# The weights' largest values by a matmul with ones, raw weights loaded a matrix ahead, hints for the tails' branches, and the last tail at the end

## The chip, the core and the metric

The kernel runs on one core of one Trainium2 chip. Its time is that of one execution on the device, in microseconds (us). The time before is the median of three runs, and a profile is taken of one further execution. The core's engines are called TensorE or PE (matmuls; PEld is its weight load), VectorE or DVE, ScalarE or ACT, GpSimd or POOL, and SyncE or SP, which here only issues DMAs.

## What is computed

Attention without softmax over 8 batches, 8 heads, 576 positions and 64 columns per head, a norm, and then a mixture of 8 experts over the 4608 rows of 512 columns that come out, of which each row goes to two:

```python
kv = np.einsum('bhsd,bhse->bhde', k, v)
out = np.einsum('bhsd,bhde->bhse', q, kv)
rms = np.sqrt(np.mean(out * out, axis=-1, keepdims=True) + 1e-06)
x = out / rms * g_norm             # then as rows of 512
...
logits = x @ w_gate
noise_scale = np.log1p(np.exp(x @ w_noise))
noisy_logits = logits + noise_scale * noise
top2 = np.argpartition(-noisy_logits, 2, axis=1)[:, :2]
...                                 # top2_w: softmax over the two
for e in range(E):
    for k in range(2):
        mask = top2[:, k] == e
        h = np.maximum(x[mask] @ w1[e], 0.0)          # w1[e]: 512 x 1024
        out[mask] += top2_w[mask, k, None] * (h @ w2[e])   # w2[e]: 1024 x 512
```

## The kernel before, in words

**Attention** (0 to 206 us of the span). For each batch PE makes kv (L536), transposes it (L548), multiplies it with the gate's weights (L555) and then q with both (L565). A tile of 128 rows goes through six stages: s0 and s1 on ACT, s2 and s3 on ACT, DVE and POOL (L592 makes x on POOL), s5 stores x to xs in memory by a DMA that ACT issues (L601). So a late x on POOL holds ACT's queue, and what stands behind it there, kvT (L551) among others. The gate's steps run in chunks beside it (L129 to L200); in L142 to L148 DVE, ACT and POOL take turns, and PE needs the outcome gt_sel (L169) for the running counts (L179). Beside all that, expert 0's weights are made ready, and the first two units of expert 0 are begun.

**Experts** (from 206 us). An expert has 10 tiles of 128 slots. They are worked on in units: expert 0 has four full units of two tiles, the others two full units of four tiles; each expert then has a tail of the tiles 8 and 9, which are filled only in part. In the last expert the tail stands between the two full units. PE's order is written out by the loop at the end: l1 of unit u (x times w1), then l2 of unit u - 1 (h times w2). A full l1 of four tiles is 96 matmuls of 128 x 512 in f16 in eight steps of twelve, and so is its l2. A tail's l1 stands in a Switch of nine arms (called the up Switch here; L431, with the zero matmul L435 as first in each arm), one arm for each 32 columns that the expert needs; its l2 stands in a Switch of three (the down Switch). The numbers that choose the arm are loaded into PE's registers a unit ahead (RV). L893 is the Switch's own branching. At the head of an arm before already stands a hint for the arm's exit.

A unit's rows come by a gather (L344, POOL), are parted into two f16 halves, xh (L351 on ACT, L352 on POOL), and are transposed by DMAs that SP issues (xT, L364). After l1, ACT (L412) and DVE (L413) make hT of it. After l2, ACT makes y (L474) and POOL adds it to the output with an indirect DMA (L385), with a small memset, tick (L384), ahead of it.

**Weights.** While expert e is worked on, expert e + 1 is made ready in the background: fill() takes one step of locate(e + 1) and then of prepare(e + 1) at each yield of l1 and l2. locate makes the lists of rows: one-hots on DVE (L288 to L293), matmuls on PE (L301), and finish on DVE (L310 to L319). prepare makes the weights: for w1 and then for w2, SP loads 2 MB in four DMAs into the raw buffer rw (L251, L264), DVE takes the largest absolute value of each partition (mx, four reduces, L213), makes one number of each partition (sc, L215 and L217), and POOL takes the largest over the 128 partitions (al, L219). DVE makes a power of two of it (L221 to L227), and ACT and DVE (L241 to L246) part the scaled weights into two f16 halves, w1h and w1l. There is one raw buffer, so w2's load waits for the split of w1. All queues run in order, POOL's too: what stands behind L219 on POOL waits for it.

Of the kernel before, what the change touches and what calls it, by code (L numbers as in the profile page):

```python
# [9 lines left out]
F32 = mybir.dt.float32  # L10
# [5 lines left out]
OP = mybir.AluOpType  # L16
# [32 lines left out]
FE = 2  # L49
GB, HB = 6, 4  # L50
GRAIN, TY = 32, 4
PZ = 4
# [3 lines left out]
def attention_moe(ctx: ExitStack, tc: tile.TileContext, kvm, kvr, qt, gn, wgn, noise, w1, w2, out):  # L56
# [19 lines left out]
    ones = const.tile([P, P], BF, name="ones")  # L76
    V.memset(ones, 1.0)
    zrow = const.tile([P, DM], F32, name="zrow")
    V.memset(zrow, 0.0)
# [123 lines left out]

    WT = {}

    def weights(e, pool, lo, slack=0):
# [3 lines left out]
        def scale(o, src, mul):  # L210
# [7 lines left out]
            al = lists.tile([P, 1], F32, name="al")  # L218
            G.partition_all_reduce(al, sc[:, o:o + 1], channels=P, reduce_op=RED.max)  # L219
            yield  # L220
            V.tensor_scalar(al, al, 1e-30, 1e30, op0=OP.max, op1=OP.min)  # L221
            bi = lists.tile([P, 2], I32, name="bi")
# [25 lines left out]

        r1 = raw.tile([P, 4, 1024], F32, name="rw")
        for c in range(4):  # L250
            SP.dma_start(r1[:, c], w1[e, c * P:(c + 1) * P, :])  # L251
        yield WY
        for _ in range(slack):
            yield
        yield from scale(0, r1, gabs)
# [3 lines left out]
        for _ in range(min(slack, 3)):  # L259
            yield  # L260
        r2 = raw.tile([P, 4, 1024], F32, name="rw")
        v = w2[e].rearrange("(c f p) d -> c p f d", f=2, p=P)
        for c in range(4):
            SP.dma_start(r2[:, c].rearrange("p (f d) -> p f d", f=2), v[c])  # L264
        yield WY
        for _ in range(slack):
            yield
        yield from scale(3, r2, None)
# [3 lines left out]
        w["w2l"] = pool.tile([P, 4, FF], F16, name="w2l")  # L272
        yield from split(r2, w["w2h"], w["w2l"], sc[:, 4:5])
        for k in ("w2h", "w2l"):
            w[k] = w[k].rearrange("p c (f d) -> p (c f) d", f=2)
# [48 lines left out]
    for e in range(E):  # L324
        full = [[0, 1, 2, 3], [4, 5, 6, 7]] if e else [[2 * k, 2 * k + 1] for k in range(4)]
        tail = [(e, [8, 9], True)]
        full = [(e, t, False) for t in full]
        units += full + tail if e + 1 < E else full[:1] + tail + full[1:]
    XG, XT, HT, RV = {}, {}, {}, {}
    late = {}  # L330
    rot = [0]
# [62 lines left out]
    def l1(u):  # L394
# [35 lines left out]
        pss = [ps_tile([P, 2, 256]) for _ in range(4)]  # L430
        for arm in tc.Switch({ET.PE: RV[e][0]}, 256 // GRAIN + 1):  # L431
            n = arm * GRAIN
# [12 lines left out]
    def l2(u):  # L445
# [10 lines left out]
        if tail:  # L456
            pss = [ps_tile([P, DM]) for _ in tiles]
            for arm in tc.Switch({ET.PE: RV[e][1]}, len(tiles) + 1):
                for i, ps in enumerate(pss):
                    if i < arm:  # L460
                        mms(ps, i, range(8))
                    else:
                        T.matmul(ps, zero[:, 0:P], zero, start=True, stop=True)  # L463
# [256 lines left out]
    late["moe"] = after.enter_context(tc.tile_pool(name="moe_b", bufs=1))  # L720
    wts_b = after.enter_context(tc.tile_pool(name="wts_b", bufs=1))
    late["ps"] = ctx.enter_context(tc.tile_pool(name="psb", bufs=4, space=PSUM))
    psl = ctx.enter_context(tc.tile_pool(name="psl", bufs=1, space=PSUM))
# [71 lines left out]
    for u in range(EARLY, len(units) + 1):  # L795
        if u < len(units):
# [19 lines left out]
            todo = deque([halves, xpose] if u + 1 < len(units) and u + 1 not in XT else ())  # L816
            for i, _ in enumerate(l1(u)):
                fill()
                if todo and i >= XH:
                    todo.popleft()(u + 1)  # L820
            while todo:
                todo.popleft()(u + 1)
        if u > EARLY:
            for _ in l2(u - 1):
                fill()
# [71 lines left out]
```

## Time and profile before

| | |
|---|---|
| three runs | 1015.4, 1013.5, 1014.5 us |
| their median | 1014.5 us |
| the profiled execution | 1018.11 us, span 1016.3 us |
| mean granted clock of PE | 0.962 |
| PE busy | 916.7 us, 90% of the span |
| DVE, POOL, ACT busy | 491.0, 393.7, 330.9 us |
| moved by DMA | 146.01 MB, 144 GB/s on the mean |

The profile is of one execution, which took 3.6 us longer than the median of the runs. Busy times are those of the instructions alone; the idle time in front of an instruction is put down to what released it. A line number is one of kernel.py as printed above; a line such as L407 covers many matmuls, which differ in shape.

### The profile page before, as it was taken

How to read it: one execution, taken by the hardware profiler on the slowest of the kernel's cores; microseconds unless marked ns; L12 is line 12 of the kernel's file. 1: busy time of each engine (PE TensorE's matmuls, PEld its weight loads, DVE VectorE, ACT ScalarE, POOL GpSimd, SP SyncE). 2: the span in 40 equal slices, each digit the busy share in tenths (PEclk: the TensorE clock that was granted, in tenths of full speed). 3: DMA queues.
4: the chain of work that ended last, by engine and by line, in shares of the span. 5: the costliest groups of instructions: out<-in, count | busy, mean ns of one | idle time of the engine just before them, and what ended most of it. 6: DMA issues, size and time to landing. Idle time of an engine off the chain costs nothing. (4 is left out here: it accounts for less than half of the span.)

```text
span 1016.3 us, 15038 instructions
## 1 busy us (share of the span) xinstructions
PE 916.7 (90%) x5930; PEld 515.9 (51%) x5930; DVE 491.0 (48%) x1013; ACT 330.9 (33%) x573; POOL 393.7 (39%) x414
## 2 busy tenths in 40 slices
PE   9785877897879899999999999999998889998996
PEld 8674865584334544445444544464443344644442
DVE  2667998752735345454535443544255355411010
ACT  1645654222422242224323322332234223422221
POOL 0214454534441454236422552247213732452412
PEclk9995899998999999999999999999999999999998
DMA  9893986785563654554545474537255755462504
GB/s 344 300 349 132 335 283 225 226 168 125 120 108 109 160 81 95 146 126 97 114 103 155 97 127 94 163 79 145 44 141 131 137 93 170 91 116 56 94 10 59
DMA packets 140835, 146.01 MB, mean 144 GB/s; under 512 B 90785, under 2 KB 99105, under 8 KB 140705
## 3 DMA queue, kind: packets, MB, share of 16 engines
q1 hardware_dynamic: 108192, 82.25, 29.0%
q0 software_dynamic: 17920, 41.95, 22.2%
q10 hardware_dynamic: 14592, 19.93, 5.9%
q8 instruction: 99, 1.62, 0.7%
q14 instruction: 32, 0.25, 0.1%
HBM read 83.02 MB, written 40.11 MB: 121 GB/s over the span
## 5 line engine op out<-in xcount | busy, mean ns | idle before, releaser
L407 PE MATMUL pp<-xT,w1h 128*128 128x512 f16 (+5 forms) x1600 | 368.5, 328 | 20.2 <-DMA xT<-xh 14.1
L453 PE MATMUL pp<-w2h,hT 128*128 128x512 f16 x1200 | 364.0, 381 | 12.1 <-issue 4.6
L453 PEld LDWEIGHTS <-hT 128*128 128x128 f16 x1800 | 175.2, 98 | 226.0 <-issue 14.1
L413 DVE SCALAR_TENSOR_TENSOR hT<-pp,hT 128x512 f16<-128x512 f32 x160 | 107.4, 687 | 334.7 <-ACT hT L412 334.1
L407 PE MATMUL pp<-xT,w1l 128*128 128x512 f16 (+5 forms) x800 | 257.6, 327 | 0.0
L385 POOL DMA_INDIRECT out_rows<-y,row x80 | 133.6, 1670 | 255.5 <-ACT y L474 234.9
L453 PE MATMUL pp<-w2l,hT 128*128 128x512 f16 x600 | 228.7, 381 | 0.0
L407 PEld LDWEIGHTS <-w1h 128*128 128x128 f16 x1600 | 152.1, 100 | 128.1 <-issue 26.4
L412 ACT ACTIVATE hT<-pp 128x512 f16<-128x512 f32 x160 | 92.4, 597 | 302.0 <-PE pp L407 292.5
L352 POOL TENSOR_TENSOR xh<-xg,xh 128x512 f16<-128x512 f32 x80 | 113.6, 1444 | 115.5 <-ACT xh L351 93.4
L474 ACT ACTIVATE y<-pp,gate 128x512 f32<-128x512 f32 x80 | 53.7, 683 | 213.4 <-PE pp L453 198.1
L407 PEld LDWEIGHTS <-w1l 128*128 128x128 f16 x800 | 80.0, 100 | 56.0 <-issue 2.5
L213 DVE TENSOR_REDUCE mx<-rw 128x1 f32<-128x1024 f32 x64 | 76.8, 1215 | 63.3 <-DMA rw<-w 63.1
L344 POOL DMA_INDIRECT xg<-xs,idx x80 | 83.4, 1043 | 33.4 <-issue 21.7
L592 POOL TENSOR_TENSOR x<-o,ss 128x512 f32<-128x512 f32 x36 | 38.7, 1077 | 58.0 <-DVE ss L586 44.4
L565 PE MATMUL big<-kvbd,qt 128*128 128x160 f32 (+1 forms) x320 | 59.1, 335 | 1.9 <-ACT kvbd L557 1.9
L351 ACT ACTIVATE xh<-xg 128x512 f16<-128x512 f32 x80 | 46.7, 623 | 23.1 <-DMA xg<-xs,idx 16.0
L565 PEld LDWEIGHTS big<-kvbd,qt 128*128 128x128 f32 (+1 forms) x320 | 49.7, 200 | 4.6 <-ACT kvbd L557 3.0
L288 DVE TENSOR_TENSOR oa<-jb,lnb 128x1152 bf16<-128x1152 bf16 x32 | 50.9, 1591 | 0.6 <-PE M L301 0.6
L219 POOL PARTITION_ALL_REDUCE al<-sc x16 | 6.2, 390 | 115.4 <-DVE sc L217 73.9
L241 ACT ACTIVATE w1h<-rw,sc 128x1024 f16<-128x1024 f32 x32 | 34.9, 1139 | 30.1 <-DVE sc L227 30.0
L241 ACT ACTIVATE w2h<-rw,sc 128x1024 f16<-128x1024 f32 x32 | 35.0, 1137 | 24.5 <-DVE sc L224 24.5
(130 smaller groups left out, 594.0 us busy)
## 6 DMA issues: line engine op xcount, KB each, us to landing
rw<-w SPq DMA_DIRECT2D x64, 512.0 KB, 6.6
kvc<-kvm SPq DMA_DIRECT2D x32, 512.0 KB, 7.8
xs<-x ACTq DMA_DIRECT2D x36, 256.0 KB, 3.9
out_rows<-zrow ACTq DMA_DIRECT2D x36, 256.0 KB, 2.5
qt<-qt SPq DMA_DIRECT2D x8, 640.0 KB, 6.2
qt<-qt SPq DMA_DIRECT2D x8, 512.0 KB, 7.1
kvr<-kvr SPq DMA_DIRECT2D x4, 512.0 KB, 8.6
xg<-xs,idx POOLq DMA_INDIRECT x80, 4.1
```

The source lines that it names most:

```text
L213: V.tensor_reduce(mx[:, c:c + 1], src[:, c], axis=AX.X, op=OP.max, apply_absolute_value=True)
L241: A.activation(hi[:, c], src[:, c], AF.Copy, scale=s)
L288: V.tensor_tensor(oa, jb[:, None, :].to_broadcast([P, n, P]), lnb[:, s, e:e + 1].to_broadcast([P, n, P]), OP.is_equal)
L344: G.indirect_dma_start(out=x, out_offset=None, in_=src, in_offset=bass.IndirectOffsetOnAxis(ap=LI[e][:, t:t + 1], axis=0))
L352: G.tensor_tensor(x[:, 1], XG[u, t], x[:, 0], OP.subtract)
L385: d = G.indirect_dma_start(out=out, out_offset=bass.IndirectOffsetOnAxis(ap=LS[e][:, t:t + 1], axis=0), in_=y, in_offset=None, compute_op= ...
L407: T.matmul(ps[:, f % ps.shape[1], 0:n], w[wn][:, c, f * P:(f + 1) * P], x[:, xo + c, 0:n], start=(c == 0 and k == 0), stop=(c == HP - 1 an ...
L412: A.activation(h[:, 0, f:f + nf, 0:n], ps, AF.Relu)
L413: V.scalar_tensor_tensor(h[:, 1, f:f + nf, 0:n], ps, 0.0, h[:, 0, f:f + nf, 0:n], op0=OP.max, op1=OP.subtract)
L453: T.matmul(ps, h[:, hk, f, i * P:(i + 1) * P], w[wn][:, f], start=(f == 0 and k == 0), stop=(f == 7 and k == 2))
L474: A.activation(y, ps, AF.Copy, scale=LG[e][:, t:t + 1])
L565: T.matmul(TL[t, "ps"][r0:r0 + n, hp, 0:160], q[:, hp, s0 - o:s0 - o + n], kvbd[b % 2][:, hp, :], start=True, stop=True)
```

## The change

Five edits:

1. POOL's all-reduce over the partitions goes. DVE writes sc onto the diagonal of a 128 x 128 tile (dg = ident times sc), two background steps later PE multiplies a tile of ones (onef) with it, in f32, which gives each partition the whole row of 128 values, and a step later DVE takes the largest of these.
2. There are two raw buffers, one for w1 (pool raw) and one for w2 (raw_b). Both matrices of expert 1 are loaded right after attention. From then on w1 of expert e + 1 is loaded when w1 of expert e has been split, and w2 likewise, so each load goes out a matrix ahead of where it did.
3. The Switches carry labels, and switch_hint names them: at the sixth step of the l2 that stands before an up Switch, and at the sixth step of the l1 before a down Switch.
4. The last expert's tail stands behind both of its full units.
5. The buffers of xg are five instead of six. A dictionary moves up, and an import goes.

The diff, cut to its core:

```diff
@@ imports, constants
-from concourse.bass_isa import ReduceOp as RED
-GB, HB = 6, 4
-GRAIN, TY = 32, 4
+GB, HB = 5, 4
+GRAIN, TY, HINT = 32, 4, 5
+onef = const.tile([P, P], F32, name="onef")
+V.memset(onef, 1.0)
@@ before weights(), and in scale()
-    WT = {}
+    WT, RW, late = {}, {}, {}
+
+    def load_w1(e):
+        r = RW[e, 0] = raw.tile([P, 4, 1024], F32, name="rw")
+        for c in range(4):
+            SP.dma_start(r[:, c], w1[e, c * P:(c + 1) * P, :])
+
+    def load_w2(e):
+        r = RW[e, 1] = late.get("raw", raw).tile([P, 4, 1024], F32, name="rw")
+        v = w2[e].rearrange("(c f p) d -> c p f d", f=2, p=P)
+        for c in range(4):
+            SP.dma_start(r[:, c].rearrange("p (f d) -> p f d", f=2), v[c])
...
             al = lists.tile([P, 1], F32, name="al")
-            G.partition_all_reduce(al, sc[:, o:o + 1], channels=P, reduce_op=RED.max)
-            yield
+            dg = lists.tile([P, P], F32, name="dg", bufs=1)
+            V.tensor_scalar(dg, ident, sc[:, o:o + 1], None, op0=OP.mult)
+            yield
+            yield
+            ps = ps_tile([P, P])
+            T.matmul(ps, onef, dg, start=True, stop=True)
+            yield
+            V.tensor_reduce(al, ps, axis=AX.X, op=OP.max)
             V.tensor_scalar(al, al, 1e-30, 1e30, op0=OP.max, op1=OP.min)
@@ in weights(), behind split()
-        r1 = raw.tile([P, 4, 1024], F32, name="rw")
-        for c in range(4):
-            SP.dma_start(r1[:, c], w1[e, c * P:(c + 1) * P, :])
-        yield WY
-        for _ in range(slack):
-            yield
+        if (e, 0) not in RW:
+            load_w1(e)
+            yield WY
+            for _ in range(slack):
+                yield
+        r1 = RW.pop((e, 0))
         yield from scale(0, r1, gabs)
...
-        r2 = raw.tile([P, 4, 1024], F32, name="rw")
-        v = w2[e].rearrange("(c f p) d -> c p f d", f=2, p=P)
-        for c in range(4):
-            SP.dma_start(r2[:, c].rearrange("p (f d) -> p f d", f=2), v[c])
-        yield WY
-        for _ in range(slack):
-            yield
+        if (e, 1) not in RW:
+            load_w2(e)
+            yield WY
+            for _ in range(slack):
+                yield
+        elif e + 1 < E:
+            load_w1(e + 1)
+        r2 = RW.pop((e, 1))
         yield from scale(3, r2, None)
...
         yield from split(r2, w["w2h"], w["w2l"], sc[:, 4:5])
+        if "raw" in late and e + 1 < E:
+            load_w2(e + 1)
@@ units
-        units += full + tail if e + 1 < E else full[:1] + tail + full[1:]
+        units += full + tail
@@ l1(), l2()
-        for arm in tc.Switch({ET.PE: RV[e][0]}, 256 // GRAIN + 1):
+        for arm in tc.Switch({ET.PE: RV[e][0]}, 256 // GRAIN + 1, hint=f"up{e}"):
...
-            for arm in tc.Switch({ET.PE: RV[e][1]}, len(tiles) + 1):
+            for arm in tc.Switch({ET.PE: RV[e][1]}, len(tiles) + 1, hint=f"down{e}"):
@@ behind attention
+    late["raw"] = after.enter_context(tc.tile_pool(name="raw_b", bufs=1))
+    load_w1(1)
+    load_w2(1)
@@ the loop over the units
             for i, _ in enumerate(l1(u)):
+                if i == HINT and u and units[u - 1][2]:
+                    tc.switch_hint({ET.PE: RV[units[u - 1][0]][1]}, 3, label=f"down{units[u - 1][0]}")
                 fill()
...
-            for _ in l2(u - 1):
+            for i, _ in enumerate(l2(u - 1)):
+                if i == HINT and u + 1 < len(units) and units[u + 1][2]:
+                    en = units[u + 1][0]
+                    tc.switch_hint({ET.PE: RV[en][0]}, 256 // GRAIN + 1, label=f"up{en}")
+                if i == HINT and u + 1 == len(units):
+                    tc.switch_hint({ET.PE: RV[e][1]}, 3, label=f"down{e}")
                 fill()
```

On POOL, in attention, the rows of before from the first x on (L592 is x; L219 the all-reduce, whose ISA rows are its setup, as L147's is; L147 and L148 are the gate's):

```order
L592 TENSOR_TENSOR x<-o,ss 128x512
L219 ISA
L219 ISA al<-sc 128x1
L592 ISA
L592 TENSOR_TENSOR x<-o,ss 128x512 x8
L219 ISA
L219 ISA al<-sc 128x1
L147 ISA
L147 TENSOR_TENSOR gt_w<-gt_w,gt_nl 128x72
L148 TENSOR_TENSOR gt_w<-gt_w,nz 128x72
```

The same place on POOL in the changed kernel, where x is L612 and the gate's are L148 and L149:

```order
L528 MEMSET kvbd_162 128x640
L612 TENSOR_TENSOR x<-o,ss 128x512 x9
L148 TENSOR_TENSOR gt_w<-gt_w,gt_nl 128x72
L149 TENSOR_TENSOR gt_w<-gt_w,nz 128x72
L612 TENSOR_TENSOR x<-o,ss 128x512 x2
```

Both all-reduces and the setup rows around them are gone, and the x and the gate's instructions follow each other directly.

On SP, one expert's period among the experts, before (L364 is xT, two for a tail and eight for two full units; L251 and L264 are the loads of w1 and w2; L893 is a Switch):

```order
L364 DMA_TRANSPOSE xT<-xh 128x8x128 x2
L251 DMA rw<-w 128x1024 x4
L264 DMA rw<-w 128x2x512 x4
L893 UNCONDITIONAL_BRANCH
L364 DMA_TRANSPOSE xT<-xh 128x8x128 x8
L893 UNCONDITIONAL_BRANCH
```

and in the changed kernel (L384 is xT; L210 and L216 are the loads; L923 is a Switch):

```order
L384 DMA_TRANSPOSE xT<-xh 128x8x128 x2
L210 DMA rw<-w 128x1024 x4
L923 UNCONDITIONAL_BRANCH
L216 DMA rw<-w 128x2x512 x4
L384 DMA_TRANSPOSE xT<-xh 128x8x128 x8
L923 UNCONDITIONAL_BRANCH
```

The load of w2 has moved behind the up Switch, where it stands directly ahead of the eight transposes of the next full units; it is that of an expert later than before.

On PE, in the l1 of a second full unit of the changed kernel (L427 is the matmul of l1, L236 the one with ones):

```order
L427 LDWEIGHTS w1h
L427 MATMUL pp<-xT,w1h 128x512
L427 LDWEIGHTS w1l
L427 MATMUL pp<-xT,w1l 128x512
L236 MATMUL pp<-dg,onef 128x128
L427 LDWEIGHTS w1h
L427 MATMUL pp<-xT,w1h 128x512
```

Before, nothing of the weights' preparation stood on PE; now the matmul with ones stands between two of l1's steps.

On PE, in the l2 before an up Switch of the changed kernel (L473 is the matmul of l2, L852 the hint):

```order
L473 LDWEIGHTS hT
L473 MATMUL pp<-w2h,hT 128x512
L852 SWITCH_STRIDE
L852 ISA
L852 BRANCH_PREFETCH_HINT
L473 LDWEIGHTS hT
L473 MATMUL pp<-w2h,hT 128x512
```

The three rows of L852 are new. From them to the Switch itself there are 122 rows on PE, 61 matmuls with their weight loads.

More of the change, by code (lines that the diff above doesn't have):

```diff
@@ L327, in attention_moe @@
         full = [(e, t, False) for t in full]
-        units += full + tail if e + 1 < E else full[:1] + tail + full[1:]
+        units += full + tail
     XG, XT, HT, RV = {}, {}, {}, {}
-    late = {}
     rot = [0]
```

## The prediction

> **What bounds the kernel now.** I read the page's busy times, then the waits of PE in two stretches, then POOL's timeline at those waits, the records of the Switches' branches, and the granted clock in windows. On the page:
>
> ```profile
> span 1016.3 us, 15038 instructions
> PE 916.7 (90%) x5930; PEld 515.9 (51%) x5930; DVE 491.0 (48%) x1013; ACT 330.9 (33%) x573; POOL 393.7 (39%) x414
> ```
>
> PE is busy for 90%, so only its idle time and its slow time can be won. Waits of PE from 20 to 206 us (attention), in us, times, longest:
>
> ```profile
> PE RM L179 <- DVE gt_sel L169: 17.0, 2, 11.9
> PE kvt L555 <- ACT kvT L551: 11.8, 4, 6.9
> ```
>
> and from 206 to 1010 us (the experts):
>
> ```profile
> PE pp L407 <- DMA xT<-xh: 14.1, 3, 7.3
> PE pp L435 <- issue: 6.2, 3, 2.4
> PE pp L407 <- issue: 6.1, 4, 3.5
> PE pp L453 <- issue: 4.6, 2, 3.4
> PE pp L435 <- DVE mx L213: 4.5, 2, 2.4
> PE pp L453 <- ACT hT L412: 3.4, 2, 2.1
> PE M L301 <- DVE ob L293: 3.4, 1, 3.4
> PE pp L435 <- DVE sc L215: 2.7, 1, 2.7
> ```
>
> L435 is the first matmul in an arm of an up Switch. Its 13.4 us are three rows with three names; the names are chance, the place is one. Who is late in the other rows is seen on POOL (its timeline: start, duration, idle before):
>
> ```profile
> 34.72 0.38 POOL L219 PARTITION_ALL_REDUCE al<-sc  x1 [5.84 <-issue]
> 45.65 2.04 POOL L592 TENSOR_TENSOR x<-o,ss 128x512 f32<-128x512 f32 x2 [10.55 <-issue]
> 70.24 0.38 POOL L219 PARTITION_ALL_REDUCE al<-sc  x1 [9.10 <-issue]
> 79.64 0.33 POOL L147 TENSOR_TENSOR gt_w<-gt_w,gt_nl 128x72 f32<-128x72 f32 x1 [9.02 <-issue]
> 231.67 0.38 POOL L219 PARTITION_ALL_REDUCE al<-sc  x1 [7.02 <-issue]
> 239.12 2.98 POOL L352 TENSOR_TENSOR xh<-xg,xh 128x512 f16<-128x512 f32 x2 [7.07 <-ACT y L474]
> ```
>
> Each all-reduce itself takes 0.38 us, but POOL stands idle 6 to 9 us before it and 7 to 10.5 us behind it. The wait of 11.9 us follows the second, since L147, L148 and the chain to gt_sel come after it; the one of 6.9 us follows the first (x late, so ACT's store waits, and kvT stands behind it on ACT). The xT wait of 7.3 us follows the third: xh stands behind it on POOL, and SP's transpose behind xh.
>
> The Switches' branches (duration in ns, start):
>
> ```profile
> L893 PEldq COMPARE_BRANCH  x1: 6281/6281/6281, 342.6 to 342.6; - x1
> L893 PEldq COMPARE_BRANCH  x1: 3521/3521/3521, 395.9 to 395.9; - x1
> L893 PEldq COMPARE_BRANCH  x1: 301/301/301, 406.1 to 406.1; - x1
> ```
>
> The first is an up Switch, where PE then idles; the second a down Switch, whose 3.5 us lie under matmuls already queued (PE has no wait there); the third is an arm's exit, which already carries a hint at the arm's head, and takes 0.3 us. The two waits of L453 <- issue are the exits of expert 5's empty tail, too short for any hint: they stay.
>
> Waits cost twice: behind them PE runs at half clock (us, busy times of PE, PEld, DVE, ACT, POOL, granted clock, DMA share, GB/s):
>
> ```profile
> 49.40:54.40 5.00, 4.97 (x25) 4.86 (x26) 4.83 (x12) 3.17 (x9) 1.94 (x2) 0.50 0.28 97
> 85.00:88.50 3.50, 3.50 (x16) 2.95 (x16) 3.30 (x8) 3.47 (x7) 2.15 (x5) 0.50 0.40 150
> 242.20:249.00 6.80, 3.19 (x30) 3.12 (x30) 0.00 (x0) 0.00 (x0) 5.52 (x6) 0.50 1.18 204
> 300.20:307.00 6.80, 4.79 (x12) 1.75 (x13) 0.00 (x0) 0.00 (x0) 2.18 (x3) 0.50 0.71 143
> 559.60:563.00 3.40, 3.37 (x30) 3.26 (x31) 1.38 (x2) 0.00 (x0) 1.13 (x3) 0.50 0.63 84
> 798.50:801.90 3.40, 3.40 (x9) 1.18 (x8) 0.00 (x0) 0.55 (x1) 2.79 (x3) 0.50 1.09 149
> 100.00:125.00 25.00, 22.08 (x259) 20.01 (x259) 23.10 (x100) 15.27 (x41) 12.55 (x17) 0.82 0.91 323
> ```
>
> **Removing the all-reduce, attention.** The two waits, 11.9 + 6.9 = 18.8 us, end if POOL goes straight on. Half clock behind them: half of 5.0 and of 3.5, 4.3 us. Ceiling 23. What is late next are DVE and the DMA engines: in 100 to 125 us DVE is busy 23.1 of 25 us and the DMA share is 0.91, so work pulled forward meets full engines there. I take 18; the floor is 8, if that stretch takes back all but a third.
>
> **Removing it, experts.** Of the three xT waits (14.1) the smallest, 0.8, follows no all-reduce and stays, and of the 6.0 behind the second I leave 1.3 for branch and register loads that come with it: 12.0. The issue row's longest, 3.5, stands at 794 us behind another all-reduce, since its xh is late in the same way: together 15.5. The ob wait of 3.4 goes, since its chain on DVE stood behind the same result. Half clock: PE is busy 3.19 + 4.79 + 3.37 + 3.40 = 14.75 us in the four windows at 0.50, half of which is 7.4.
>
> The Trainium skill, "TensorE: Matmul & The Clock Gate", section "Part 1: The HAM clock gate", has the clock fall to half only after at least one idle window of about 3.4 us. The window at 559.6 follows a wait of 2.4 us alone, so the trace disagrees on that; by the page 1.7 us of the 7.4 would not be the wait's.
>
> **Hints.** The new hint stands at the sixth step of the l2 before an up Switch, some 60 matmuls ahead, where the branch took 6.3 us. If it is then like the hinted exit's 0.3 us, all 13.4 us of L435 go. The hint for the down Switch in the l1 wins nothing at its entry, which is hidden now; the two L453 waits at exits (3.4) I count as gone: they stand where an exit comes too soon after its hint, and with the tail's l2 now fetched ahead the sequencer is further in front. Experts' sum so far: 15.5 + 3.4 + 7.4 + 13.4 + 3.4 = 43.1 us.
>
> **What is added.** On PE, fourteen matmuls of 128 columns in f32 among the experts. The nearest row:
>
> ```profile
> 60.53 1.35 PE L565 MATMUL big<-kvbd,qt 128*128 128x160 f32 x8
> ```
>
> Each matmul is recorded twice there, so four in 1.35: 0.34 us for 160 columns, 0.27 for 128; 14 x 0.27 = 3.8. Below nothing it cannot be, since PE is the bound.
>
> PE is in order, so the matmul also waits for dg, and all of l1's steps are queued behind it. For w1 of each next expert this falls in the second full unit's l1, where locate's end stands ahead on DVE:
>
> ```profile
> 419.59 0.20 DVE L310 COPY m<-M 128x50 f32<-128x50 f32 x1
> 422.91 0.68 DVE L413 SCALAR_TENSOR_TENSOR hT<-pp,hT 128x512 f16<-128x512 f32 x1
> 424.16 0.69 DVE L413 SCALAR_TENSOR_TENSOR hT<-pp,hT 128x512 f16<-128x512 f32 x1 [0.56 <-ACT hT L412]
> 426.75 0.69 DVE L413 SCALAR_TENSOR_TENSOR hT<-pp,hT 128x512 f16<-128x512 f32 x1 [1.90 <-ACT hT L412]
> 430.40 0.68 DVE L413 SCALAR_TENSOR_TENSOR hT<-pp,hT 128x512 f16<-128x512 f32 x1
> 431.00 2.33 DVE L213 TENSOR_REDUCE mx<-rw 128x1 f32<-128x1024 f32 x2
> 433.25 0.68 DVE L413 SCALAR_TENSOR_TENSOR hT<-pp,hT 128x512 f16<-128x512 f32 x1
> 433.85 0.14 DVE L215 TENSOR_REDUCE sc<-mx 128x1 f32<-128x4 f32 x1
> ```
>
> A step of PE is 426.75 - 424.16 = 2.6 us. Raw weights are there early now, so DVE is the late one: locate's end 3.3 (419.59 to 422.91), hT 0.6, two reduces 2.3, hT 0.6, two reduces 2.3, hT 0.6, and about 0.6 for sc, gabs and dg (the first is 0.14): 10.3 us. It begins some 1.3 us (an ACT and a DVE hT, 0.6 + 0.7) behind its step on PE, and PE gets to the matmul four steps, 10.4, later. Wait 10.3 + 1.3 - 10.4 = 1.2 us, for six experts 7. It is nothing if locate's end is quicker than here, and up to 3 for each of all fourteen matmuls (a rival, below).
>
> **Raw weights ahead.** DVE's reduces no longer wait for loads; that is worth nothing on PE, where no wait of this kind stands outside the Switches. But SP's queue changes: the w2 load now goes out once the split of w2 is done, ahead of the eight transposes xT of the next expert's first full units. Its price as it stands:
>
> ```profile
> L264 SPq DMA_DIRECT2D rw<-w x4: 379/462/467, 441.9 to 443.3; - x4
> DMA to landing us min/median/max: 5.3/7.7/11.4
> 937.02 2.06 ACT L412 ACTIVATE hT<-pp 128x512 f16<-128x512 f32 x4 [6.16 <-PE pp L407]
> ```
>
> From 441.9 to the last landing 443.3 + 11.4 = 454.7 are 12.8 us. I estimate that it goes out some 5 us after a tail's arm ends (four hT, 2.1 us, then the rest of the split), so it is through at 18. The transposes land behind it, from about 21 to 23. PE needs them when the l2 that follows the arm is done: 96 matmuls, as in a full l1, so eight steps of 2.6, 20.8 us. So about 2 us a time for four experts: 8, from 0 (transposes pass the load) to 15.
>
> **Last tail at the end.** Its two y and scatters stand behind the last matmul instead of one. A scatter with its tick is about 2 us longer on POOL than the chain is now: 2, from 1 to 4. GB, late and the import cost nothing.
>
> **Sum.** Experts: 43.1 - 3.8 - 7 - 8 - 2 = 22.3. With attention's 18 it is 40 us. The profiled execution took 1018.1 us, so 978; the runs' median is 1014.5, 3.6 below it: 975 (974.5 rounded).
>
> **Rivals.**
> 1. The hints do nothing (the change doesn't do what it says). The sequencer runs through a hundred straight instructions between hint and branch and may lose the page fetched. Then 13.4 and 3.4 stay: 992. Against it: the hinted exit of 0.3 us lies 10 us behind its hint too. The Trainium skill, "Runtime: NRT & Kernel Launch", section "Instruction fetch mechanics", has the fetch purely sequential and each taken branch outside the window a forced fetch; by that rule this rival holds. The 0.3 us speaks against it. Chance 0.18.
> 2. Attention shortens by 8 only, since DVE and DMA are full at 100 to 125 us: 985. Chance 0.14.
> 3. Each of the fourteen scale matmuls waits 3 us for dg instead of the six with 1.2, because raw loads or hT hold DVE: 42 in place of 7, so 1010. For it: the same DVE queue takes hT for PE. Against: only w1's reduces stand behind locate. Chance 0.10.
> 4. Slower: the transposes stand behind the w2 load longer. The sum without (i.e. with the 8 given back) is 967; from 9.5 us a time for five experts it is 1014.5, and from there on the change loses. With 11 us a time, and 1.7 us of half clock behind each wait, it is 1030. Against it: the load would have to go out some 12.5 us behind the arm, or take 20 us where it took 12.8. Chance 0.03.
>
> **How the numbers follow.** The forecast, 975, has 0.55, and its own bounds are: below, no dg wait, no xT wait and attention's ceiling, 7 + 8 + 5 = 20, so 955, and 5 of scatter: 950; above, xT at 15 and dg doubled: 989. Rivals 1 and 2 lie within 998 with some 6 us of scatter; 3 and 4 are left out with 0.13. So 950 to 998. Two us, 0.2%, is about what a measurement of this kernel can tell from no change. All cases but the fourth are faster; from the third I give 0.02 to no change: faster 0.95, same 0.02, slower 0.03.
>
> **What would show it.** In the changed profile: no idle of 6 us on POOL in attention, and the gt_sel and kvT waits under 2 us; up Switches' branches at 0.3 us and no wait at the zero matmul; xT waits of about 2 us behind the up Switches; a wait of about 1 us at the scale matmul in the second full unit. Wrong it would be with branches of 6 us in the up Switches, with waits of over 2 us at scale matmuls, or with xT waits of 5 us and more.

## The result and the profile after

The changed kernel takes 1018.86 us, the median of 20 runs (1007.36 to 1026.38), and the kernel before, beside it on the same chips, 1010.31 us, the median of 20 as well (1004.85 to 1015.4). The ratio is 1.007, with a 95% interval of 1.0047 to 1.0093: the change makes the kernel slower, and the forecast was 975. The ratios here and below are estimates with their intervals, not quotients of the medians, and leave out slow executions, of which the changed kernel has three (the profiled one is among them). The profiled executions stand above these medians, before by 7.8 us (1018.11) and after by 4.6 (1023.48), so differences between the two traces are read by stage and not from the ends.

The page of the changed kernel, its span and busy times:

```profile
span 1021.6 us, 15198 instructions
PE 920.9 (90%) x5962; PEld 516.6 (51%) x5962; DVE 497.8 (49%) x1046; ACT 331.1 (32%) x573; POOL 379.6 (37%) x398
```

PE's share is the same 90%: what the edits took away in waits came back as other waits. Those of 20 to 206 us, in us, times, longest:

```profile
PE big L585 <- ACT kvbd L577: 12.5, 4, 9.9
PE kvt L575 <- ACT kvT L571: 6.4, 5, 2.0
PE RM L180 <- DVE gt_sel L170: 5.1, 1, 5.1
```

and those from 206 us on:

```profile
PE pp L427 <- DMA xT<-xh: 28.7, 5, 8.2
PE pp L236 <- DVE dg L232: 8.6, 6, 1.5
PE pp L427 <- issue: 5.1, 3, 2.5
PE pp L236 <- DVE hT L433: 3.6, 1, 3.6
PE pp L455 <- DVE dg L232: 1.5, 1, 1.5
```

The waits of 11.9 us (gt_sel) and 6.9 us (kvT) are gone, but a new one of 9.9 us stands in attention, and the first unit behind attention starts only 4.7 us earlier (at 201.5 us instead of 206.2). Among the experts the zero matmuls (L455) wait for 1.5 us in place of 13.4; the matmul with ones waits 8.6 us in six places; and the waits for xT have doubled, to 28.7 us. The branch of an up Switch where PE waited before, in ns:

```profile
L923 PEldq COMPARE_BRANCH  x1: 308/308/308, 440.6 to 440.6; - x1
```

So the hint does what it says there, and it does so at the other up Switches from 327 us on, which take 0.31 to 0.41 us (expert 5's, whose tail is empty, takes 0.3 us without a hint as well). It does not at the first, in expert 0, where it stands only 2.4 us ahead of the Switch:

```profile
L923 PEldq COMPARE_BRANCH  x1: 4994/4994/4994, 229.9 to 229.9; - x1
```

Four of the five xT waits, 6.8, 6.4, 8.2 and 5.3 us, stand behind the load of w2 (the fifth, 2.1 us at 259, does not). This is seen on SP's DMA issues at 570 us (issue, duration; then how long from issue to landing, min, median, max), first the load, then the transposes behind it, then four transposes that stand behind no load:

```profile
L216 SPq DMA_DIRECT2D rw<-w x4: 379/468/469, 569.8 to 571.2; - x4
DMA to landing us min/median/max: 3.7/5.1/6.5
...
L384 SPq DMA_TRANSPOSE xT<-xh x4: 1573/3242/5116, 571.8 to 580.1; - x4
PE pp L427: 8.2, 1
DMA to landing us min/median/max: 8.0/11.5/12.1
...
L384 SPq DMA_TRANSPOSE xT<-xh x4: 1232/1250/1287, 604.8 to 609.8; - x4
DMA to landing us min/median/max: 3.1/3.2/3.2
```

Behind the load a transpose takes 11.5 us to land instead of 3.2, and even its issue takes 3.2 us instead of 1.25. The fourth is issued at 580.1 and lands 12.1 us later, at 592.2; PE, at 584.2, waits for it for 8.2 us. The DMA queues (packets, MB, share of the 16 engines) show what runs meanwhile; q1 carries what SP issues, q0 the scatters and gathers that POOL issues. In the changed kernel, 569.7 to 578:

```profile
q1 hardware_dynamic: 1505, 2.20, 88.0%
```

and 578 to 592.3:

```profile
q1 hardware_dynamic: 3807, 0.94, 74.5%
q0 software_dynamic: 597, 1.17, 49.3%
```

In the kernel before, at the same place, 577 to 584.4:

```profile
q1 hardware_dynamic: 4083, 1.02, 71.7%
```

The load's 2 MB go first; about a tenth of the four transposes' 1 MB has moved by 578. The rest takes 14 us beside scatters and gathers, where before all of it took 7 us with no other queue at work, since the scatters came behind it. A packet of the transposes takes some 45 ns instead of 21 (an estimate: share times 16 engines times the stretch, by the packets). So the load has an effect that outlasts it: it moves the transposes to where they meet the scatters.

And PE pays again (us, busy times, granted clock), in the four windows behind the waits of 5 to 8 us; the fifth window follows a wait of 2.5 us (L427 <- issue), the last two follow waits of 1.5 and 1.4 us at the matmul with ones:

```profile
365.90:369.40 3.50, 3.50 (x9) 1.24 (x9) 0.00 (x0) 0.00 (x0) 0.88 (x1) 0.50 0.86 319
480.00:483.50 3.50, 3.50 (x9) 1.18 (x8) 0.00 (x0) 0.00 (x0) 0.95 (x1) 0.50 0.80 286
592.40:595.80 3.40, 3.40 (x9) 1.20 (x10) 0.00 (x0) 0.00 (x0) 0.00 (x0) 0.50 0.66 260
700.60:704.00 3.40, 3.40 (x9) 1.18 (x8) 0.00 (x0) 0.00 (x0) 1.90 (x2) 0.50 0.83 253
804.90:808.30 3.40, 3.40 (x10) 1.20 (x9) 0.00 (x0) 0.24 (x1) 2.48 (x4) 0.50 0.92 196
533.70:537.00 3.30, 3.30 (x16) 1.65 (x17) 1.39 (x7) 0.22 (x1) 0.00 (x0) 1.00 0.00 0
850.40:853.00 2.60, 2.60 (x13) 1.31 (x14) 1.34 (x7) 0.00 (x0) 0.00 (x0) 1.00 0.00 0
```

Half clock behind the four xT waits costs half of 13.8, 6.9 us. The new wait in attention begins on DVE (start, duration, idle before):

```profile
64.58 1.22 DVE L225 TENSOR_REDUCE mx<-rw 128x1 f32<-128x1024 f32 x1 [9.45 <-DMA rw<-w]
```

DVE comes to the reduce of expert 0's w2 at 55.1 us, before the load is issued, and stands there for 9.45 us, with ACT and PE behind it. In the trace of before the load went out at 51.4 and DVE came to it at 57.6, with no wait:

```profile
51.44 3.00 SPq L264 DMA_DIRECT2D rw<-w  x4
57.57 1.21 DVE L213 TENSOR_REDUCE mx<-rw 128x1 f32<-128x1024 f32 x1
```

In the changed kernel it goes out at 55.6:

```profile
55.59 3.86 SPq L216 DMA_DIRECT2D rw<-w  x4
```

It stands two steps later in the program, since scale has two more yields, and so behind the next batch's loads of k and v on SP, while POOL, no longer held, lets DVE arrive earlier. Two runs below bear out that the yields do this: in the kernel before with the first edit alone the loads of k and v go out at 46.1 us, w2's at 54.4, and DVE waits for it for 8.25 us; with the all-reduce and its single yield back, w2's load goes out at 50.5, ahead of those of k and v at 55.4.

### The profile page after: what moved, and what is told of

The parts are those of the page before. It is cut to its first block, busy times and chain, and to the rows that moved or that the text cites. A ratio compares the mean times of both kernels' runs of the same rounds, so it can differ in the third digit from the quotient of the medians.

```text
span 1021.6 us, 15198 instructions
## 1 busy us (share of the span) xinstructions
PE 920.9 (90%) x5962; PEld 516.6 (51%) x5962; DVE 497.8 (49%) x1046; ACT 331.1 (32%) x573; POOL 379.6 (37%) x398
## 5 line engine op out<-in xcount | busy, mean ns | idle before, releaser
L427 PE MATMUL pp<-xT,w1h 128*128 128x512 f16 (+5 forms) x1600 | 370.2, 329 | 36.1 <-DMA xT<-xh 28.7
L473 PE MATMUL pp<-w2h,hT 128*128 128x512 f16 x1200 | 364.8, 381 | 1.9 <-ACT hT L432 1.2
L473 PEld LDWEIGHTS <-hT 128*128 128x128 f16 x1800 | 176.0, 98 | 212.8 <-issue 5.4
L405 POOL DMA_INDIRECT out_rows<-y,row x80 | 130.1, 1626 | 371.5 <-ACT y L494 354.6
L427 PE MATMUL pp<-xT,w1l 128*128 128x512 f16 (+5 forms) x800 | 257.5, 328 | 0.0
L473 PE MATMUL pp<-w2l,hT 128*128 128x512 f16 x600 | 228.7, 381 | 0.0
L427 PEld LDWEIGHTS <-w1h 128*128 128x128 f16 x1600 | 150.6, 99 | 147.2 <-issue 49.4
L427 PEld LDWEIGHTS <-w1l 128*128 128x128 f16 x800 | 79.5, 99 | 58.0 <-issue 5.8
L364 POOL DMA_INDIRECT xg<-xs,idx x80 | 79.9, 998 | 35.1 <-issue 23.0
L225 DVE TENSOR_REDUCE mx<-rw 128x1 f32<-128x1024 f32 x64 | 74.4, 1208 | 11.3 <-DMA rw<-w 11.3
L612 POOL TENSOR_TENSOR x<-o,ss 128x512 f32<-128x512 f32 x36 | 38.6, 1073 | 64.6 <-DVE ss L606 57.4
L585 PEld LDWEIGHTS big<-kvbd,qt 128*128 128x128 f32 (+1 forms) x320 | 49.3, 201 | 17.3 <-ACT kvbd L577 13.4
L404 POOL MEMSET tick<- 1x1 f32 x80 | 37.2, 465 | 0.0
```

What stands on the lines that cost most here:

```text
L225: V.tensor_reduce(mx[:, c:c + 1], src[:, c], axis=AX.X, op=OP.max, apply_absolute_value=True)
L364: G.indirect_dma_start(out=x, out_offset=None, in_=src, in_offset=bass.IndirectOffsetOnAxis(ap=LI[e][:, t:t + 1], axis=0))
L405: d = G.indirect_dma_start(out=out, out_offset=bass.IndirectOffsetOnAxis(ap=LS[e][:, t:t + 1], axis=0), in_=y, in_offset=None, compute_op= ...
L427: T.matmul(ps[:, f % ps.shape[1], 0:n], w[wn][:, c, f * P:(f + 1) * P], x[:, xo + c, 0:n], start=(c == 0 and k == 0), stop=(c == HP - 1 an ...
L473: T.matmul(ps, h[:, hk, f, i * P:(i + 1) * P], w[wn][:, f], start=(f == 0 and k == 0), stop=(f == 7 and k == 2))
L585: T.matmul(TL[t, "ps"][r0:r0 + n, hp, 0:160], q[:, hp, s0 - o:s0 - o + n], kvbd[b % 2][:, hp, :], start=True, stop=True)
```

## The experiments

The kernel before was timed beside each; its median there was 1007.6 to 1012.4 us, so a difference of a few us between two experiments is uncertain unless the ratios show it too. The theory after the traces: the loss among the experts is the second edit's load of w2 ahead of the transposes; attention's lost gain is the load of expert 0's w2; the first, third and fourth edit are sound. The rivals are in the expectations. In each diff the changed kernel is the base, unless it says otherwise.

**w2's load put behind the transposes**, at the head of weights(e), ahead of w1's reduces:

```diff
         yield from split(r2, w["w2h"], w["w2l"], sc[:, 4:5])
-        if "raw" in late and e + 1 < E:
-            load_w2(e + 1)
...
+        if "raw" in late and (e, 1) not in RW:
+            load_w2(e)
         r1 = RW.pop((e, 0))
```

> The changed kernel, with the load of w2 of expert e+1 issued at the start of weights(e+1), behind the transposes, instead of ahead of them. Theory (the transposes queue behind that load on SP): PE's waits for xT fall from 28.7 us to under 4, the half clock behind them goes, and the time falls by about 33 us. Rival (the transposes are slow because scatters and gathers share the DMA engines then): xT waits stay over 15 us, and the time falls by less than 12 us.

982.16 us, ratio to before 0.9723 (0.9663 to 0.9784), 36.7 us under the changed kernel. Its waits for xT:

```profile
PE pp L236 <- DVE dg L232: 8.6, 6, 1.6
PE pp L427 <- DMA xT<-xh: 3.5, 1, 3.5
```

One issue moved by half an expert is worth 25.2 us of waits and the half clock behind them. The theory holds as to what has to move. It doesn't say by which way the load hinders the transposes, and it doesn't exclude the rival's scatters and gathers: with the load moved, the transposes run ahead of the scatters again, as in the kernel before.

**Six more steps in attention before the reduce of w2.**

```diff
             load_w2(e)
             yield WY
-            for _ in range(slack):
+            for _ in range(slack + 6):
                 yield
```

> The changed kernel, with six more steps between expert 0's load of w2 and its first reduce, in attention. Theory (DVE stands at the reduce for a load that is not there yet, 9.5 us, and PE behind it): that wait of DVE and PE's 9.9 us at 70 us go, and the time falls by about 10 us. Rival (attention is bound by its loads by then): the wait comes back elsewhere in attention, and the time falls by 3 us or less.

1035.89 us, ratio 1.024 (1.0176 to 1.0305): a miss, 17 us slower than the changed kernel. In its trace attention's wait of 9.9 us is gone, and the kernel is 7 us ahead at 228 us; then the xT waits are

```profile
PE pp L427 <- DMA xT<-xh: 47.8, 5, 20.8
```

instead of 28.7, with one of 20.8 us. How long the transposes take behind the load thus differs from kernel to kernel, and what makes it 20.8 us there isn't shown. The edit has to be judged where they don't, below.

**The same load from ACT's queue.**

```diff
-            SP.dma_start(r[:, c].rearrange("p (f d) -> p f d", f=2), v[c])
+            (A if "raw" in late and e > 1 else SP).dma_start(r[:, c].rearrange("p (f d) -> p f d", f=2), v[c])
```

> The changed kernel, with the load of w2 ahead issued by ACT instead of SP, at the same place of the program, so at about the same time. Theory A (the transposes only stand behind the load in SP's queue): xT waits fall under 6 us and the time falls by 25 us or more, as with the load put behind. Theory B (the load takes the DMA engines that the transposes need, whatever the queue): xT waits stay over 15 us, and the time falls by less than 12 us.

1006.83 us, ratio 0.9978 (0.9945 to 1.0012), 12 us under the changed kernel by the medians and 9 by the ratios, with xT waits of 19.0 us in its list. By these totals theory B holds; place by place it is between the two. Four transposes right behind the load, now on another queue, one expert ahead of the place shown above:

```profile
L384 SPq DMA_TRANSPOSE xT<-xh x4: 1263/1752/3267, 469.0 to 475.1; - x4
DMA to landing us min/median/max: 4.9/5.5/5.8
```

5.5 us to landing, against 3.2 alone and 11.5 behind the load on the same queue. The four waits that were 6.8, 6.4, 8.2 and 5.3 us are 2.5, 0.5, 2.5 and 0.9 us here, but a fifth, 2.1 before, is 15.2 us. There the last transpose was issued at 256.3, in the midst of the four loads (255.3 to 256.8), and landed at 272.0; from 262 us on scatters and gathers were under way as well. So both rivals have a part: the order in SP's queue has the larger one in four places, and sharing the DMA engines, without that order, can hold a transpose for 15.7 us. How much of this is the load and how much the scatters and gathers stays open; beside scatters alone, at 475 to 481 us, the transposes of the rows above kept landing in 5 to 6 us.

**Without hints, and the hints alone.** The changed kernel without the labels and the three switch_hint calls, of which the diff shows one:

```diff
-        for arm in tc.Switch({ET.PE: RV[e][0]}, 256 // GRAIN + 1, hint=f"up{e}"):
+        for arm in tc.Switch({ET.PE: RV[e][0]}, 256 // GRAIN + 1):
...
-                if i == HINT and u + 1 < len(units) and units[u + 1][2]:
-                    en = units[u + 1][0]
-                    tc.switch_hint({ET.PE: RV[en][0]}, 256 // GRAIN + 1, label=f"up{en}")
```

> The changed kernel without the three switch_hint calls and the labels. Theory (the hint makes the branch short): up Switches' branches take 4 to 6 us again, PE waits about 10 to 13 us at the zero matmuls, and the time rises by 10 to 17 us. Rival (the branches were long only because w2's load ran at the same time, and it doesn't now): branches under 3.6 us, hidden, and a time within 4 us of the changed kernel.

1032.3 us, ratio 1.0232 (1.0155 to 1.0309), 13 us slower, but not for the reason that was expected. An up Switch's branch there:

```profile
L916 PEldq COMPARE_BRANCH  x1: 3707/3707/3707, 561.7 to 561.7; - x1
```

3.7 us, hidden: PE waits 1.3 us at the zero matmuls. The xT waits are 32.4 us instead of 28.7, and the exits wait some 5 us; the rest of the 13 us stays open. By its time the rival fails too, which allowed 4 us. About the entry it fits: without w2's load beside them the up Switches' branches of the experts 1 to 4 and 6 take 3.3 to 3.7 us, and with it, in the kernel before, 5.7 to 6.3. The kernel before with the labels and the first two hint calls alone (base: the kernel before, with L435 and L453 as before and L898 as the Switch):

```diff
-            for _ in l2(u - 1):
+            for i, _ in enumerate(l2(u - 1)):
+                if i == HINT and u + 1 < len(units) and units[u + 1][2]:
+                    en = units[u + 1][0]
+                    tc.switch_hint({ET.PE: RV[en][0]}, 256 // GRAIN + 1, label=f"up{en}")
                 fill()
```

> The kernel before with the labels and the hints alone. If the hint makes the branch short also beside w2's load: no wait at the zero matmuls (L435, 13.4 us before) and a time 10 to 17 us below before. If it does not there: within 4 us of before.

986.26 us, ratio 0.9813 (0.9719 to 0.9906), 23 us faster by the medians, more than expected, but by the interval anything from 9 to 28 us. Its branch at an up Switch, beside w2's load:

```profile
L898 PEldq COMPARE_BRANCH  x1: 312/312/312, 437.8 to 437.8; - x1
```

Of the five up Switches that took 5.7 to 6.3 us, three are like this. At the other two the branch takes 3.1 and 3.8 us although its hint stands some 13 us ahead, one of them:

```profile
L898 PEldq COMPARE_BRANCH  x1: 3818/3818/3818, 637.0 to 637.0; - x1
```

PE has no wait there either. Its waits at the zero matmuls from 325 us on:

```profile
PE pp L435 <- issue: 1.2, 1, 1.2
PE pp L435 <- PE pp L453: 0.2, 1, 0.2
```

Of the 13.4 us 1.4 are left, and the half clock that followed is gone. The xT wait of 6.1 us at 302, behind a down Switch, is 2.3 here. Not all of the 23 us need be the hints': in the trace the first unit behind attention starts at 202.2 us instead of 206.2, and no hint stands ahead of it. The first edit alone loses, as shown below, and the fourth is worth little; the second was not run alone. So of the edits that were, the third is the only gain.

**No load ahead.** The changed kernel without its second edit: no raw_b, no load_w1 and load_w2 after attention, none ahead in weights().

```diff
-    late["raw"] = after.enter_context(tc.tile_pool(name="raw_b", bufs=1))
-    load_w1(1)
-    load_w2(1)
...
-        elif e + 1 < E:
-            load_w1(e + 1)
```

> The changed kernel without its second edit: no load ahead, one raw buffer as before. If the load ahead is the whole loss among the experts, the time is some 25 us or more below the changed kernel, under 992 us. If the matmul with ones is a loss of its own (dg late on a load that is not there yet, with all of l1 behind it), waits at L236 of over 15 us, and a time of over 1000 us.

1021.16 us, ratio 1.0143 (1.0076 to 1.021): no faster than with the load ahead, so the second expectation holds. The xT waits are gone, and instead:

```profile
PE pp L236 <- DVE dg L232: 34.4, 11, 5.0
```

One of the 5 us on the timelines of DVE and PE (start, duration, idle before):

```profile
666.44 1.21 DVE L225 TENSOR_REDUCE mx<-rw 128x1 f32<-128x1024 f32 x1
667.68 0.16 DVE L227 TENSOR_REDUCE sc<-mx 128x1 f32<-128x4 f32 x1
667.88 0.54 DVE L232 TENSOR_SCALAR dg<-ident,sc 128x128 f32<-128x128 f32 x1
...
668.56 0.55 PE L236 MATMUL pp<-dg,onef 128*128 128x128 f32 x1 [4.90 <-DVE dg L232]
```

The load's last piece has just landed, DVE reduces it, and PE stands in its order at the matmul. So the first edit is a loss without the second. The kernel before with the first edit alone (base: the kernel before):

```diff
-            G.partition_all_reduce(al, sc[:, o:o + 1], channels=P, reduce_op=RED.max)
+            dg = lists.tile([P, P], F32, name="dg", bufs=1)
+            V.tensor_scalar(dg, ident, sc[:, o:o + 1], None, op0=OP.mult)
+            yield
             yield
+            ps = ps_tile([P, P])
+            T.matmul(ps, onef, dg, start=True, stop=True)
+            yield
+            V.tensor_reduce(al, ps, axis=AX.X, op=OP.max)
```

> The kernel before with the first edit alone: the matmul with ones in place of the all-reduce, and the loads where they were. If the matmul needs the loads ahead (its dg waits for a load just issued, as without the second edit, 34 us of waits there): 10 to 30 us slower than before, with over 30 us of waits at the matmul with ones. By the prediction's sum for this edit (xT and gate waits gone, 10.8 us paid): 20 us or more faster than before.

1043.71 us, ratio 1.0327 (1.0254 to 1.0399), with 36.5 us of waits for dg; also the zero matmuls wait 14.1 us, without hints. The expectation that came from these waits holds, with the size a little over it, and the prediction's sum for the edit alone fails by over 50 us.

**Three edits together.** w2's load behind the transposes, the six steps, and one more step before the matmul with ones:

```diff
             V.tensor_scalar(dg, ident, sc[:, o:o + 1], None, op0=OP.mult)
             yield
             yield
+            yield
```

> The changed kernel with three edits: w2's load behind the transposes, six more steps in attention before the reduce of w2, and one more step between dg and the matmul with ones. If the three prices add (33, 10 and the 8.6 us of waits for dg), the time is about 50 us below the changed kernel, near 968 us. If attention's loads bind and dg's wait only moves, it is 35 us below.

965.15 us, ratio 0.9551 (0.9498 to 0.9605), 53.7 us below the changed kernel: the prices add about as expected, and this kernel is 4.5% faster than before. Two runs then gave the price of each of the last two, with the same diffs on the kernel with w2's load behind the transposes. The six steps:

> The changed kernel with w2's load behind the transposes (982 us) and six more steps in attention before expert 0's reduce of w2: the edit of the run that was 17 us slower, now without the transposes behind a load. If attention's lost gain was DVE's wait for that load (8 us earlier at the end of attention in that run's profile): 7 to 11 us faster than 982. If the wait only moves to DVE's other work: within 3 us of 982.

974.13 us, ratio 0.964 (0.9573 to 0.9707), 8.0 us under 982.16. PE's waits for kvbd in attention fall from 13.5 to 2.5 us, so DVE's wait for the load was a loss of about that size; the first unit behind attention starts 5.3 us earlier (193.0 instead of 198.3), and smaller waits take the rest. And the one step more before the matmul:

> The changed kernel with w2's load behind the transposes (982 us) and one more step between dg and the matmul with ones. If dg is late by 1.4 us in six of l1's (8.6 us of waits): those waits go, 7 to 9 us faster than 982. If the matmul's other waits (for hT, for the reduce behind it) take their place: within 3 us.

969.42 us, ratio 0.9609 (0.9537 to 0.968), 12.7 us under 982.16, more than the 8.6 us of waits; the one xT wait of 3.5 us is gone here too, and the first unit behind attention starts 2.8 us earlier. Together they are 20.7 us, and 17.0 in one kernel. The largest waits that remain among the experts in the kernel with all three edits:

```profile
PE pp L237 <- ACT hT L433: 3.9, 1, 3.9
PE pp L428 <- issue: 3.7, 4, 1.3
```

**Hints, all-reduce, tail and more steps, on that kernel.** Without any hint (the diff is that of the run without hints above):

> The kernel with the three edits (965 us) without any hint, where no load of w2 runs beside an up Switch. Theory (a branch without hint is 3.6 us there and hidden under queued matmuls, as in the changed kernel without hints): at most 6 us slower than with hints, most of it at exits and short arms. Rival (the hints are worth what the waits at L435 were): 13 us or more slower.

971.82 us, ratio 0.9635 (0.9573 to 0.9697), 6.7 us slower, a little over what the theory allowed: by the medians hints are worth 23 us beside w2's load and 7 us away from it. With POOL's all-reduce back:

```diff
-            dg = lists.tile([P, P], F32, name="dg", bufs=1)
-            V.tensor_scalar(dg, ident, sc[:, o:o + 1], None, op0=OP.mult)
...
-            T.matmul(ps, onef, dg, start=True, stop=True)
...
-            V.tensor_reduce(al, ps, axis=AX.X, op=OP.max)
+            G.partition_all_reduce(al, sc[:, o:o + 1], channels=P, reduce_op=RED.max)
+            yield
```

> The kernel with the three edits (965 us), with POOL's all-reduce in place of the matmul with ones. If the matmul's gain is POOL's idle time, as the prediction had it: 15 to 30 us slower, with xT waits of over 10 us and a gate wait of about 10 us in attention back. If a load ahead already takes the all-reduce off the path (its input is early): within 6 us.

998.71 us, ratio 0.9884 (0.985 to 0.9919), 34 us slower. POOL's idle time is back, with xT waits as expected; the gate's wait is not (gt_sel stays at 5.1 us), and kvbd's is there instead. Here it stands before the second all-reduce in attention, on POOL's timeline, and below it are PE's longest wait in attention and the xT waits:

```profile
82.95 0.38 POOL L232 PARTITION_ALL_REDUCE al<-sc  x1 [10.03 <-issue]
```

```profile
PE big L580 <- ACT kvbd L572: 16.1, 2, 15.3
...
PE pp L422 <- DMA xT<-xh: 20.6, 2, 17.5
```

Nearly all of it lies in attention and expert 0: behind 290 us PE has only three waits of over 1 us, 3.1 at most. With loads a matrix ahead the all-reduce is off the path for the later experts. The steps of this kernel had been placed for the matmul; whether other places would serve the all-reduce better was not tried. With the last tail between the full units:

```diff
-        units += full + tail
+        units += full + tail if e + 1 < E else full[:1] + tail + full[1:]
```

> The kernel with the three edits (965 us), with the last expert's tail between its full units as before. If the fourth edit is worth its two us at the end and no more, in the other direction: 0 to 3 us faster than with the tail last. If the tail at the end saves the waits around it (1.5 and 2.1 us before): up to 3 us slower. Over 4 us either way speaks against both.

963.53 us, ratio 0.9533 (0.9472 to 0.9593), 1.6 us faster, which the intervals cannot tell from nothing. With four more steps ahead of the matmul with ones in attention, where PE waits 7.8 us in the kernel with the three edits (slack is 2 there and 0 among the experts):

```diff
             V.tensor_scalar(dg, ident, sc[:, o:o + 1], None, op0=OP.mult)
-            yield
-            yield
-            yield
+            for _ in range(3 + 2 * slack):
+                yield
```

> The kernel with the three edits (965 us), with four more steps between dg and its matmul in attention alone, where PE waits 7.8 us for dg at 81 us. If that wait is a matter of order on PE: 5 to 9 us faster. If DVE is the bound there (it is busy without a gap from 60 to 84 us): the wait moves, and the time is within 2 us.

974.03 us, ratio 0.9639 (0.9565 to 0.9714), 9 us slower: a miss for both. The wait is gone, but DVE's other work, one-hots and the gate's counts, then comes later:

```profile
PE RM L322 <- DVE ob L314: 8.3, 4, 4.7
PE kvt L568 <- ACT kvbd L564: 4.8, 3, 3.0
```

That fits DVE as the bound there, with a later step making it worse.

## Why the prediction was wrong, point by point

- **Hints** (13.4 + 3.4 us): right in the mechanism for the entries. The branch is 0.31 us, L455's waits are 1.5 us. The Trainium skill, "Runtime: NRT & Kernel Launch", section "Instruction fetch mechanics", would have had the branch as long as before; the measured 308 ns against 6.3 us decides against that for a hinted branch. Alone the hints are worth 23 us by the medians, more than their terms; the sum has half clock behind L435 at 559.6 us only, and the trace of before has it at 662.0 too. The 3.4 us at exits were not sound: the prediction first says that these two waits stay and then counts them as gone, the row has 4.6 us for the two and 3.4 for the longest alone, and with the hints alone that one is still 3.1 us.
- **dg late** (1.2 us for six experts, 7): right, 8.6 us in six places, 1.5 at most. A wait of 3.6 us for hT at the same matmul had no term. Nor was it priced what the matmul costs without the loads ahead: 34 us of waits.
- **The matmuls' own time** (3.8 us): in the trace of the changed kernel the fourteen among the experts, 28 records of L236, keep PE busy for 5.9 us. PE's busy time as a whole rose by 4.2 us, with 32 more records.
- **xT behind w2's load** (8 us, 0 to 15): here the prediction failed. The place was right, and the slower rival had this very mechanism, at a chance of 0.03. The size was not: I let the transposes follow a finished load at their usual pace, in 3 to 5 us. The load itself was no slower than assumed (2 MB through by 578 us, 8 us behind its first issue, where the sum took 12.8). But in the trace a transpose takes 11.5 us from issue to landing, and the last lands 14 us behind the end of the load, beside scatters and gathers that came behind it before. Which part of that is due to the scatters, and which to the queue, stays open. The four waits behind the load are 26.7 us, and half clock adds 6.9: 33.6 in place of 8, and putting the load elsewhere gave back 36.7. The rival's own price, 9.5 us a time for five experts, was not reached either (5.3 to 8.2 us in four): the change loses only because attention fell short as well.
- **Attention** (18 us, floor 8): here it failed a second time. The two waits are gone as forecast, but the first unit of the experts after attention starts 4.7 us earlier (201.5 against 206.2 us), below the floor too. I named DVE and the DMA engines as late next at 100 to 125 us, and the wait came at 70 us instead, for a load that two more yields had put behind others on SP. In the prediction that load and the yields have no term at all: an edit that adds a step also moves each DMA issue that comes after it. Six steps gave back 8.0 us of the 13.3 that are missing; the rest stays open.
- **Half clock** (7.4 us among the experts): gone at 300 and 559.6 us; still there behind L427's issue wait (804.9 us, 798.5 before) and in expert 0 (245.1, 242.2 before); and back behind the xT waits. The Trainium skill, "TensorE: Matmul & The Clock Gate", section "Part 1: The HAM clock gate", asks for some 3.4 us of idleness; waits of 5 to 8 us here were followed by it and waits of 1.5 us not, which agrees, while the 2.4 us in the trace of before does not, and neither does the 2.5 us ahead of 804.9 us in that of the changed kernel.
- **The tail at the end** (2 us): 1.6 us, within what can't be told from nothing.
- **The sum.** 975, and 13.3 us of attention and 25.6 us of xT on top, is 1014; the median is 1018.9. The two steps account for most of the miss. What is left is 5 us here, and 9 from the median of the 20 executions of the kernel before (1010.3, where the sum began at 1014.5); the 3.6 us wait for hT and the 2 us too little for the matmuls are of that order, but no run separates them.

The range was set as if the terms were independent. The term that needed the wide end was the one whose both ends came from a load with nothing behind it in its queue.

## What to carry to other kernels

A prefetch that goes out earlier is not free: look at what it now stands ahead of in its queue and which small, urgent transfers share the engines with it, and put the load behind these. An added step moves each later issue in a hand-written order, and a queue's order may turn over. Price edits in pairs as well as alone: here the matmul with ones lost 33 us without the loads ahead and won 34 us with loads that were well placed, nearly all of it in attention and expert 0.

## What the runs showed of the hardware

- A branch of PE at an up Switch with a hint some 60 matmuls (13 us) ahead took 0.31 to 0.41 us in the changed kernel from expert 1 on; with a hint 2.4 us ahead it took 4.99. Without a hint it took 3.3 to 3.7 us in the changed kernel's experts 1 to 4 and 6, and 5.7 to 6.3 us in those of the kernel before, where a load of 2 MB ran beside it. With the hint and that load it took 0.31 to 0.32 us in three of these places and 3.1 and 3.8 in two; and one down Switch with a hint, at 921 us in the changed kernel, took 3.5.
- A transposing DMA landed in 3.2 us alone, in 5.5 us right behind a 2 MB load from another queue, in 11.5 us behind it on the same queue (beside scatters and gathers from 579 us on), and in 15.7 us when it was issued in the midst of such a load from another queue.
- What the same transposes cost changed from 28.7 to 47.8 us with six steps more in attention, the longest wait of them 500 us later: a wait of this kind is not a constant to be carried from one kernel to the next.
